# New orders for every engine's list and for the PSUM pairs of a fused gated SSM-convolution and mixer kernel

## The chip, the cores and the metric

The kernel runs on one core of one Trainium2 chip. The metric is the device time of one execution in microseconds (us), median of several runs; lower is better. The profile is one more execution, recorded by the hardware profiler. In its rows PE is the matrix engine (TensorE), PEld its weight loads, DVE the vector engine, ACT the scalar engine, POOL the GpSimd engine and SP the engine whose queue issues most DMA transfers; a q behind an engine's name is its sequencer, which waits and issues.

## The reference

```python
def _A_ref(q, k, v, shift_k, ssm_k, ssm_D):
    ...
    for t in range(ks):
        k_shift = k_shift + k_pad[:, t:t + S, :] * shift_k[:, ks - 1 - t][None, None, :]
    kv = k_shift * v
    ...   # y: causal convolution of kv with ssm_k along the sequence, through rfft / irfft
    y = y + kv * ssm_D[None, None, :]
    return q * y

def _B_ref(x, w1, w2, w3, w4):
    h = _gelu(_layernorm(x, axis=-1) @ w1)
    ...   # hs: four column groups of h shifted by +1, -1, +2, -2 rows, then @ w2
    x1 = x + hs
    h2 = _gelu(_layernorm(x1, axis=-1) @ w3) @ w4
    return x1 + h2

x = A_q
g = _sigmoid((x * gate_w).sum(-1, keepdims=True))
return g * a + (1 - g) * b      # a = _A_ref(x, ...), b = _B_ref(x, ...)
```

S is 2048, D 640, F 1536, all in bfloat16. Branch A is a gated long convolution; branch B is a two-layer mixer; a sigmoid gate per row mixes them.

## The kernel before, in words

The 2048 rows lie in SBUF as 2 blocks (c) x 8 residue classes (rho or r) x 128 partitions. Everything is written as 981 nodes, each one instruction or a short run of matmuls on one engine, with its reads and writes. `schedule(RANK, PAIR)` then sorts all nodes by a rank from a written-out table, `RANK`, and each engine works through its nodes in that order, without looking ahead. A node waits on semaphores for what it depends on on other engines; everything behind it on that engine waits too. So the table sets the order of each engine's list.

PSUM is four pairs of banks. Each matmul job (a node or two on PE, and the ACT or DVE instruction that evicts it) has its pair from a second table, `PAIR`. A job's first node waits until the job before it on that pair has been evicted.

The names of nodes that matter here, with the line that records the operation:

- fill: up to 96 matmuls on a tile of ones (L645), whose result nobody reads; those that are last in PE's list are dropped.
- shk: row broadcasts of the shift taps on PE (L656), evicted by ACT. gwt (L651) and gsum (L909) are small products for the gate, halo (L667) makes the rows before a block.
- bn (L776 statistics, L778 aggregate), ln (small DVE instructions at L554, L766, L768, L794) and the reciprocal root on POOL (L756): layer norm, once for x, once for x1. For the first, class 1 has its statistics from ACT. Classes 2 and 3, 4 and 5, 6 and 7 share a root. The second is in four groups, with row sums by ACT and squares by ACT (L566, with the accumulator read).
- xn: the normalised rows (DVE L554, or ACT L566 for most of the second norm). xTp (L821): transposition on PE of a class's normalised rows, evicted by ACT (xTe). Classes 6 and 7 of the first norm and all of the second are transposed by DMA from SP's queue.
- mm1 (L861): first product of B with gelu, by pairs of classes; the first pair is split into class 0 and class 1, each in three pieces. tail (L901): small DMAs from POOL's queue that shift the fifth column tile. mm2 (L971, seeded in PSUM by ACT at L953), mm3 (L1062, gelu on ACT) and mm4 (L1033, seeded) are the other products. The last group of mm4 is done in halves: one evicted by ACT, the other by DVE with an addition (L1046).
- kv: the four-tap convolution times v, on DVE (L549), in four parts. tap (L711): ssm_k transposed on PE. L721 is a small POOL addition of ssm_D to the taps; one comes early, one late.
- fwd (L1091): forward transform of taps (fwdh) and of kv (fwdk), for each half of the columns, evicted by ACT (Sh, Sk). DVE then does windows, butterflies, products and folds (L549), with some additions done by accumulating DMAs from POOL's queue (L1121). inv and inve (L1234) are the inverse transform, with eviction gy on ACT; fin and finx on DVE multiply by q and add to B's part.
- Stores to DRAM are issued by SP (L1273 and, for the last mm4 group, L1052), in list order.

Nearly all DVE additions and products show as L549, nearly all ACT evictions as L580, because one helper records them.

Of the kernel before, what the change touches and what calls it, by code (L numbers as in the profile page):

```python
# [292 lines left out]
def _bf16_bits(a):  # L293
# [34 lines left out]
R4M = {("h",1),("k",1)}  # L328
FILL = 96
RANK = [  # L330
# [46 lines left out]
]  # L377
PAIR = [
# [7 lines left out]
]  # L386

def _freq(kap):
# [962 lines left out]
```

## Time and profile before

| what | value |
|---|---|
| median of 3 runs | 223.71 us (223.3 to 223.88) |
| the profiled execution: time, span of its instructions | 222.89 us, 220.9 us |
| PE busy | 213.5 us, 97% |
| DVE busy | 205.9 us, 93% |
| ACT busy | 171.9 us, 78% |
| POOL busy | 58.4 us, 26% |
| granted TensorE clock | 1.00 of full speed |

Starts in the rows are microseconds from the start of the span. "[0.30 <-X]" behind a row is the time the engine stood idle before it and what ended that. Rows that follow each other on an engine with one line, operation and tile are merged (x3). Neighbouring instructions of DVE, ACT and PE overlap by about 0.1 us in the rows, since the next one starts before the last has drained.

### The profile page before, as it was taken

To read this page: it belongs to the slowest core of one execution; us is meant where nothing else is said; L and a number is where in the kernel's file an instruction comes from. 1 tells how busy PE (TensorE), PEld (TensorE's weight loads), DVE (VectorE), ACT (ScalarE), POOL (GpSimd) and SP (SyncE) were. 2 spreads that over 40 slices of the span, in tenths; PEclk is the share of its full clock that TensorE was granted. 3 is DMA by queue.
4 is the path that set the end of the run, shared out by engine and by line. 5 is a ranking of instruction groups with operands and counts; after the bars stand their busy time and mean duration, and the time that the engine had idled before them with its cause. 6 is when DMAs were issued, how large, how long until landed. Compare 5 with 4: busy or idle time off the path is not lost.

```text
span 220.9 us, 3934 instructions
## 1 busy us (share of the span) xinstructions
PE 213.5 (97%) x1531; PEld 135.5 (61%) x1531; DVE 205.9 (93%) x307; ACT 171.9 (78%) x291; POOL 58.4 (26%) x64
## 2 busy tenths in 40 slices
PE   8999999999989999999999999999999999999993
PEld 8769655557756645447765554466665577567771
DVE  2999999999999899999999999999999999984984
ACT  4798998889999999999998988855246552296561
POOL 1231780341202303490003110223231204138000
PEclk9999999999999999999999999999999999999999
DMA  6999999779976542967232450496976897798758
GB/s 216 380 399 367 360 286 188 292 151 238 184 215 197 161 82 39 346 115 235 57 59 59 74 107 0 76 156 116 184 125 119 128 323 146 141 207 117 134 159 259
DMA packets 41580, 39.76 MB, mean 180 GB/s; under 512 B 20453, under 2 KB 34792, under 8 KB 41433
## 3 DMA queue, kind: packets, MB, share of 16 engines
q1 hardware_dynamic: 33864, 24.75, 39.9%
q0 software_dynamic: 7408, 14.42, 32.3%
q10 hardware_dynamic: 288, 0.33, 0.6%
q8 instruction: 12, 0.20, 0.3%
q14 instruction: 8, 0.06, 0.1%
HBM read 21.60 MB, written 3.93 MB: 116 GB/s over the span
## 4 chain that ended last, share of the span: by engine, by line
PE 65%; DVE 19%; ACT 13%; issue 1%; DVEq 0%; ACTq 0%
PE PS L1033 23%; DVE arena L549 18%; PE PS L1062 18%; ACT arena L580 9%; PE PS L1234 7%; PE PS L1091 5%; PE PS L861 4%; PE PS L645 4%; ACT arena L566 3%; PE PS L821 2%; PE PS L711 1%; PE PS L656 1%; DVE arena L554 1%; ACT PS L953 1%; PE PS L667 0%
## 5 line engine op out<-in xcount | busy, mean ns | idle before, releaser
L549 DVE TENSOR_TENSOR arena<-arena 128x1280 bf16<-128x1280 bf16 (+5 forms) x212 | 182.8, 923 | 5.7 <-ACT arena L580 4.2
L580 ACT ACTIVATE arena<-PS 128x640 bf16<-128x640 f32 (+7 forms) x140 | 102.7, 794 | 19.6 <-PE PS L1062 11.5
L1033 PE MATMUL PS<-arena 128*128 128x320 bf16 x384 | 54.6, 299 | 0.3 <-ACT arena L580 0.3
L1062 PE MATMUL PS<-arena 128*128 128x512 bf16 x240 | 54.3, 379 | 0.1
L1033 PEld LDWEIGHTS PS<-arena 128*128 128x128 bf16 x384 | 37.5, 98 | 15.3 <-issue 0.6
L580 ACT ACTIVATE arena<-PS,arena 128x320 bf16<-128x320 f32 (+1 forms) x48 | 26.2, 594 | 21.5 <-PE PS L1033 17.2
L1121 POOL DMA_DIRECT2D arena<-arena x24 | 24.1, 1083 | 67.9 <-DVE arena L549 67.9
L1062 PEld LDWEIGHTS PS<-arena 128*128 128x128 bf16 x240 | 23.1, 98 | 26.8 <-issue 0.8
L1091 PE MATMUL PS<-arena 128*128 128x320 bf16 x208 | 33.1, 300 | 1.2 <-ACT arena L580 0.8
L1091 PEld LDWEIGHTS PS<-arena 128*128 128x128 bf16 x208 | 19.0, 98 | 13.7 <-ACT arena L580 4.4
L566 ACT ACTIVATE arena<-arena 128x640 bf16<-128x640 bf16 (+2 forms) x34 | 26.2, 776 | 1.6 <-DMA arena<-in_A_q_dram 1.2
L756 POOL TENSOR_TENSOR arena<-arena 128x4 f32<-128x4 f32 (+1 forms) x9 | 17.0, 1887 | 35.2 <-DVE arena L554 32.7
L971 PE MATMUL PS<-arena 128*128 128x320 bf16 x160 | 22.9, 299 | 1.0 <-ACT PS L953 1.0
L861 PE MATMUL PS<-arena 128*128 128x512 bf16 (+1 forms) x125 | 23.6, 336 | 0.0
L953 ACT ACTIVATE PS<-arena 128x640 f32<-128x640 bf16 x32 | 22.3, 714 | 0.3
L971 PEld LDWEIGHTS PS<-arena 128*128 128x128 bf16 x160 | 15.3, 98 | 7.7 <-issue 1.1
L861 PEld LDWEIGHTS PS<-arena 128*128 128x128 bf16 x125 | 11.7, 98 | 8.8 <-ACT arena L580 0.9
L1234 PE MATMUL PS<-arena 128*128 128x320 bf16 x112 | 17.0, 299 | 0.0
L776 DVE BATCH_NORM_STATS2 arena<-arena 128x6 f32<-128x320 bf16 x28 | 12.2, 477 | 3.4 <-DMA arena<-in_A_q_dram 3.3
L1234 PEld LDWEIGHTS PS<-arena 128*128 128x128 bf16 x112 | 10.9, 98 | 5.1 <-ACT arena L580 0.4
L901 POOL DMA_DIRECT2D arena<-arena x18 | 9.5, 536 | 9.6 <-ACT arena L580 9.6
L554 DVE TENSOR_SCALAR arena<-arena 128x640 bf16<-128x640 bf16 (+3 forms) x31 | 10.2, 349 | 1.3 <-POOL arena L756 0.8
(39 smaller groups left out, 66.0 us busy)
## 6 DMA issues: line engine op xcount, KB each, us to landing
arena<-arena POOLq DMA_DIRECT2D x18, 320.0 KB, 3.9
arena<-in_B_w_dram POOLq DMA_DIRECT2D x4, 960.0 KB, 7.1
arena<-in_A_k_dram SPq DMA_DIRECT2D x4, 640.0 KB, 7.0
arena<-in_A_v_dram SPq DMA_DIRECT2D x4, 640.0 KB, 12.9
arena<-arena POOLq DMA_DIRECT2D x4, 640.0 KB, 6.0
arena<-in_A_q_dram SPq DMA_DIRECT2D x4, 640.0 KB, 8.3
out_dram<-arena SPq DMA_DIRECT2D x15, 160.0 KB, 2.0
arena<-in_A_q_dram SPq DMA_DIRECT2D x6, 320.0 KB, 4.8
```

The source lines that it names most:

```text
L549: return dve(lambda e: e.tensor_tensor(o, a, b, op), [a, b], [o], c_tt(n), tag=tag, **kw)
L566: node = P.op("act", lambda e, ps: e.activation(o, i, func, **kw), r=r, w=[o], cost=c_act(n, naps, acc is not None, psum=False), tag=tag, ...
L580: node = P.op("act", lambda e, ps: e.activation(ov, inner(ps), func, **kw), r=r, w=[o], cost=c_act(n, len(r), acc is not None), job=job, t ...
L756: P.op("pool", lambda e, ps: e.tensor_tensor(r, v, hv, ALU.pow), r=[v, HALF], w=[r], cost=cost, tag="ln")
L861: fns.append(lambda e, ps, b=b, c=c, lhsT=lhsT: e.matmul(bank(ps, b, 256 * n), lhsT, XT[:, c, r0:r0 + n, :], start=(c == 0), stop=(c == 4)))
L953: P.seed(job, lambda e, ps: e.activation(two(ps, 320), x, ACTF.Copy), [X[:, c, rho, :]], c_act(640, psum=False), tag)
L971: fns.append(lambda e, ps, hh=hh, ft=ft, lhsT=lhsT: e.matmul(bank(ps, hh, 320), lhsT, w2v[:, ft, 320 * hh:320 * hh + 320], start=False, st ...
L1033: fns.append(lambda e, ps, hh=hh, ft=ft, lhsT=lhsT: e.matmul(bank(ps, hh, 320), lhsT, w4h[ft // 6][:, ft % 6, 320 * hh:320 * hh + 320], st ...
L1062: fns.append(lambda e, ps, b=b, ft=ft, c=c, sc=sc: e.matmul(bank(ps, b, 512), w3h[ft // 6][:, c, 128 * (ft % 6):128 * (ft % 6) + 128], XT[ ...
L1091: fns.append(lambda e, ps, w=w, b=b, rhs=rhs, st=(first and n == 0), en=(n == len(ss) - 1): e.matmul(bank(ps, b, 320), w, rhs, start=st, s ...
L1121: return P.dma("pool", lambda e, ps: e.dma_start(o, i, accum_op=ALU.add, max_dma_last_dim=2560), r=[o, i], w=[o], nbytes=nb, cost=1.2, kin ...
L1234: fns.append(lambda e, ps, w=w, z=z, c=c, st=(n == 0), en=(n == len(terms) - 1): e.matmul(bank(ps, c, 320), w, z[:, c, :], start=st, stop=en))
```

## The change

The two tables `RANK` (981 numbers) and `PAIR` (244 numbers) are replaced; the nodes, their instructions and what they read and write stay. The diff is these two tables and nothing else. Its first and last lines:

```diff
 RANK = [
-    978, 927, 967, 974, 980, 979, 966, 956, 951, 924, 932, 899, 887, 975, 938, 961, 808, 917, 797, 945, 794,
+    978, 937, 968, 975, 980, 979, 967, 952, 957, 931, 884, 924, 907, 976, 939, 962, 808, 874, 813, 946, 809,
...
 PAIR = [
-    3, 3, 3, 2, 3, 0, 0, 2, 2, 1, 2, 0, 0, 1, 1, 3, 2, 3, 1, 1, 2, 3, 1, 1, 3, 1, 2, 1, 2, 0, 3, 2, 3, 3, 3, 3,
+    2, 3, 3, 1, 1, 3, 0, 1, 1, 3, 0, 0, 0, 1, 2, 0, 2, 3, 2, 2, 3, 3, 1, 1, 2, 1, 3, 0, 0, 0, 0, 2, 0, 1, 0, 1,
...
```

Written out as lists (numbers behind a dot count the nodes of that name), these are the places that the prediction speaks of. PE's first entries:

```
before: fill x72, shk, fill x9, xTp class 0, fill x11, shk, gwt, halo 0, xTp class 1, halo 1, mm1 0a.0, mm1 0a.1, mm1 0b.2, gsum, shk, shk, mm1 0a.2, ...
after:  fill x70, shk, fill x11, shk, fill x2, gwt, xTp class 0, fill x3, halo 0, halo 1, xTp class 1, mm1 0a.0, mm1 0a.1, shk, mm1 0a.2, shk, mm1 0b.2, ...
```

DVE, from the input of the root of classes 4 and 5 on (ln 4, ln 6: inputs of the roots; statistics and aggregates are bn):

```
before: ln 4, bn x3, kv 0.1, bn, xn 5, bn x3, xn 5, bn x2, xn 4, ln 6, kv 0.0, xn 4, kv 0.2, memset, xn 6, xn 7, kv 0.3, xn 6, kv 0.4, xn 7, ...
after:  ln 4, kv 0.0, memset, bn (aggregate), xn 5, xn 5, kv 0.2, bn x2, xn 4, bn x2, xn 4, bn, ln 6, kv 0.3, memset, xn 7, xn 6, kv 0.4, xn 7, ...
```

ACT, from before the last gelu of the first mm3 group to mm4's third seed:

```
before: ..., square 3.0, gelu3, square 3.1, seed4, gelu3, Sh, gelu3, xn, seed4, xn, Sh, xn, xn, Sh, seed4, ...
after:  ..., seed4, square 3.0, gelu3, Sh, gelu3, square 3.1, seed4, Sh, xn, xn, xn, xn, Sh, Sh, seed4, ...
```

In the second norm, the reader of the root of classes 6 and 7 follows the root's input on DVE behind two butterfly instructions and a small one now, where it had four butterfly instructions and a small one before. Near the end, PE takes inve pieces 0 and 2 one behind the other after the last DVE-evicted half of a block's mm4; SP's list of stores begins with a store that needs a finx, and the two stores that went out first before are its third and twelfth now. POOL, SP and the pairs have other exchanges of neighbours.

102 rows, old and new, of tables (PAIR, RANK) are left out of this document.

## The prediction

> **What bounds the kernel now.** I read the page first (busy shares, then the chain that ended last), then the table by stage, the chain in order of time, and the timelines of single engines.
>
> ```profile
> PE 213.5 (97%) x1531; PEld 135.5 (61%) x1531; DVE 205.9 (93%) x307; ACT 171.9 (78%) x291; POOL 58.4 (26%) x64
> PE 65%; DVE 19%; ACT 13%; issue 1%; DVEq 0%; ACTq 0%
> ```
>
> PE is busy nearly always, but the chain runs through it for 65% only. The table by stage (from:to, its length; busy us and instructions of PE, PEld, DVE, ACT, POOL; granted clock, DMA share, GB/s) says where another engine is as full:
>
> ```profile
> 0.00:12.30 12.30, 11.24 (x126) 9.70 (x127) 8.23 (x30) 8.14 (x15) 2.75 (x8) 1.00 0.87 310
> 12.30:28.20 15.90, 15.90 (x166) 12.38 (x165) 15.14 (x42) 14.85 (x20) 7.13 (x7) 1.00 1.03 374
> 28.20:71.20 43.00, 41.83 (x337) 26.43 (x335) 42.50 (x30) 40.22 (x80) 12.67 (x20) 1.00 0.88 215
> 71.20:98.40 27.20, 26.25 (x151) 13.69 (x152) 26.20 (x45) 26.84 (x54) 10.64 (x8) 1.00 0.55 148
> 98.40:146.00 47.60, 47.15 (x284) 27.00 (x285) 47.29 (x63) 43.59 (x63) 6.37 (x6) 1.00 0.45 92
> 146.00:215.50 69.50, 69.50 (x466) 45.32 (x465) 64.26 (x97) 37.35 (x63) 18.80 (x19) 1.00 0.80 157
> ```
>
> From 28 to 98 us three engines are full at once. The chain in order of time (start, length, what) shows who hands over to whom:
>
> ```profile
> 1.06 6.72 PE PS L645 x72
> ...
> 8.44 0.61 PE PS L645 x9
> ...
> 9.60 0.61 PE PS L645 x11
> ...
> 28.19 1.30 DVE arena L554 x2
> ...
> 69.61 1.50 DVE arena L549
> ...
> 71.16 0.73 PE PS L1091 x4
> ...
> 71.92 1.90 ACT arena L580 x3
> ...
> 95.78 2.46 ACT arena L580 x3
> ...
> 98.37 3.42 PE PS L1033 x24
> ```
>
> So DVE decides until the last shift-convolution product ends at 71.11 (kv, L549), ACT until 98.2 (the last gelu before the first mm4), PE after that to 215.5. A list order can win only waits: no instruction is dropped but fillers. PE's idle inside 12.3 to 215.5 is 1.17 + 0.95 + 0.45 = 2.6 us (span less busy, rows three to five of the table); that and the six fillers (below) are all there is to gain before the tail.
>
> **The change, part by part.** I wrote both lists of every engine side by side, counted the work that stands ahead of each instruction in either (durations from the timelines), and looked where an input now comes after the place of its reader.
>
> *Fillers.* 92 of the L645 matmuls are issued now, 86 after. At 0.61/11 = 0.056 us each that is -0.34 us on PE, unless the next input is late. It is:
>
> ```profile
> 7.13 0.80 DVE L554 TENSOR_SCALAR arena<-arena 128x640 bf16<-128x640 bf16 x2
> 9.40 0.88 DVE L776 BATCH_NORM_STATS2 arena<-arena 128x6 f32<-128x320 bf16 x2
> 10.37 0.75 DVE L554 TENSOR_SCALAR arena<-arena 128x640 bf16<-128x640 bf16 x2
> 12.29 2.89 PE L861 MATMUL PS<-arena 128*128 128x256 bf16 x25
> ```
>
> The transposition of row class 1 stands ahead of the first mm1 piece in both lists, but DVE now does one statistics pass (0.40), one aggregate (0.11) and two memsets (0.14) more before it finishes class 1's normalised rows: 11.12 + 0.65 = 11.77 instead of 11.12. PE, 0.34 ahead, waits for it, and 0.56 of transposing later the first mm1 starts at 12.35 against 12.29. Both row broadcasts (L656) ahead of it are hidden in that wait. Net 0.0 on PE. With the cover gone (class 1 on time) it would be -0.3.
>
> *DVE to 71 us.* This is the term that matters, since DVE's end there releases fwdk. The reciprocal roots (L756) run on POOL between two DVE instructions:
>
> ```profile
> 17.94 0.49 DVE L776 BATCH_NORM_STATS2 arena<-arena 128x6 f32<-128x320 bf16 x1 [0.30 <-DMA arena<-in_A_q_dram]
> 18.58 1.01 POOL L756 TENSOR_TENSOR arena<-arena 128x4 f32<-128x4 f32 x1 [4.57 <-DVE arena L554]
> 20.99 0.20 DVE L778 BATCH_NORM_AGGREGATE arena<-arena 128x2 f32<-128x12 f32 x1
> 23.20 2.82 DVE L549 TENSOR_TENSOR arena<-arena 128x5120 bf16<-128x5120 bf16 x1
> 23.37 3.52 POOL L756 TENSOR_TENSOR arena<-arena 128x4 f32<-128x4 f32 x1 [3.79 <-DVE arena L554]
> 26.30 1.48 DVE L549 TENSOR_TENSOR arena<-arena 128x2560 bf16<-128x2560 bf16 x1
> 27.84 0.06 DVE L852 MEMSET arena<- 32x1 bf16 x1
> 28.19 1.30 DVE L554 TENSOR_SCALAR arena<-arena 128x640 bf16<-128x640 bf16 x2 [0.30 <-PE PS L821]
> 28.53 0.78 POOL L721 TENSOR_TENSOR arena<-arena 1x320 bf16<-1x320 bf16 x1
> 73.71 1.52 DVE L554 TENSOR_SCALAR arena<-arena 128x640 bf16<-128x640 bf16 x4 [0.85 <-POOL arena L756]
> 92.28 3.75 POOL L756 TENSOR_TENSOR arena<-arena 128x4 f32<-128x4 f32 x1
> ```
>
> The root takes 1.01 beside statistics passes, but 3.52 when a 2.82 us kv product starts just before it: it ends 26.89, 0.87 after the product's end at 26.02. In the old list a normalisation and the 1.48 kv step of 26.30 stand between, so nobody waits for that root. The new list has for classes 4 and 5: the root's input, the 2.82 us kv product, one memset (0.06), one aggregate (0.20 less the 0.08 by which DVE instructions overlap), and then the normalisation that needs the root. So DVE waits 0.87, plus 0.03 from POOL's end to DVE's start (73.68 to 73.71 in the row of 73.71, whose root is of the same kind), less 0.18 of small work, plus the 0.08 overlap: 0.80. For classes 6 and 7: input, a 1.48 kv step, one memset, then the reader: 0.87 + 0.03 - 0.06 + 0.08 = 0.92. Against that go the old list's own waits: 0.30 for a load (x now lands earlier), 0.30 for a transposition, 0.50 where POOL's L721 stretched two normalisations to 1.30 (0.80 at 7.13), and 0.1 of small ones. Moved work in that stretch adds 0.13. Sum 0.80 + 0.92 + 0.13 - 1.20 = +0.65: the last kv product ends at 71.76. Lower bound -0.3 (POOL slips in first and both waits vanish, the old 0.50 stays); upper bound +1.15 (L721 falls into a normalisation again). I take +0.65, nearest to the 3.52 row, which is the same pair of instructions in the same order.
>
> The Trainium skill (SBUF — State Buffer, "SBUF: two separate sides") gives the mechanism: DVE and GpSimd share one port pair, whichever starts first holds it for its whole instruction, and the other blocks. The 3.52 row agrees. By that rule alone a blocked root enters at the next instruction's end; at 92.28 it took 3.75 us beside instructions of 0.8 us, so by the row it can lose several rounds. The place where the two differ is classes 6 and 7 of the second norm (DVE about 115): by the rule its reader would wait 0.0, by the row up to 0.9, and the total would come out 0.0 or about 0.2 longer, since DVE has slack there.
>
> *ACT from 71 to 98.* fwdk starts about 71.8 instead of 71.16, so its first eviction is 0.6 late. But one square pass has been put behind the last gelu that mm4 waits for:
>
> ```profile
> 91.10 0.72 ACT L566 ACTIVATE arena<-arena 128x640 bf16<-128x640 bf16 x1
> 120.05 2.21 ACT L580 ACTIVATE arena<-PS 128x1024 bf16<-128x1024 f32 x3 [0.54 <-PE PS L1062]
> 134.70 1.62 ACT L580 ACTIVATE arena<-PS 128x1024 bf16<-128x1024 f32 x2 [0.64 <-PE PS L1062]
> 135.78 0.72 PE L1091 MATMUL PS<-arena 128*128 128x320 bf16 x4 [0.30 <-ACT arena L580]
> ```
>
> +0.6 - 0.72 = -0.1: mm4 begins at 98.25 against 98.37. PE could not be much earlier: the same work from 71.76 ends at 97.1.
>
> *98 to 146.* That square pass now stands between the gelu and everything ACT does next, so ACT is 0.6 to 0.75 behind its old place when it evicts, while PE is not. I walked the PSUM pairs by the ACT and PE timelines. An example: behind the last gelu ACT has the square (0.72), a seed, three Sh evictions, and four normalisations before mm4's third seed; that ends at 105.65, and PE stands there from 105.25. So mm4's third seed is 0.4 late, the mm3 behind Sh of the odd residue 0.35, the fwdk behind the 131 us gelu 0.55, and some 0.1s; PE's old idle here was 0.45 (the 0.30 at 135.78 among it), and ACT's own old waits (0.54, 0.64) take up most of its lag by 135. Net +0.7: inv begins 0.6 later than 145.3. Bounds: 0.0 (ACT's old waits absorb all) to +1.3 (each stall stands).
>
> *146 to the end.* PE's list is dense in both. One new wait: inve's second piece takes the PSUM pair of an mm4 half whose DVE eviction (0.55, L1046) ends 0.25 too late. PE ends about +0.9. The stores:
>
> ```profile
> 204.01 1.21 SPq L1273 DMA_DIRECT2D out_dram<-arena  x2
> 211.33 0.34 SPq L1052 DMA_DIRECT2D out_dram<-arena  x1
> 217.52 0.54 DVE L1046 SCALAR_TENSOR_TENSOR arena<-PS,arena 128x320 bf16<-128x320 f32 x1
> 218.49 0.49 SPq L1052 DMA_DIRECT2D out_dram<-arena  x1
> ```
>
> Now two stores go out at 204 and fifteen back to back from 211.33, (218.49 - 211.33)/14 = 0.51 each; the last one's data was ready at 218.06, so the queue is 0.4 late. After, all seventeen stand behind one finx that I place at 210.7, and 16 x 0.51 later is 218.9; the data is ready at 218.06 + 0.9 = 218.96. Last store +0.5.
>
> Sum on the profiled execution: 220.9 + 0.5 = 221.4 span; with the 1.99 around it (222.89 - 220.9) 223.4. The median of the runs is 223.71, 0.82 above the profiled one, so I carry +0.5 over: 224.2. About 0.3% (0.67 us) is what a measurement of this kernel tells from no change.
>
> **The rivals.** *Faster, the roots are not blocked.* If POOL gets in first both DVE waits go, fwdk starts at 71.2 and PE stays ahead by its 0.34 of fillers and some of its old 0.95 idle. The 18.58 row (1.01, unblocked) speaks for it, the 3.52 row against. PE would end 0.5 earlier, but the stores cap it: finx at 209.7, last store 217.9, so -0.6 at most: 223.1; with a little of the lag left 223.3. Chance 0.28.
>
> *Slower, ACT's lag is not recovered.* One mechanism, at 98 to 135: every PSUM pair that PE wants next is the one ACT evicts last, so PE inherits ACT's whole 0.75 and each of the stalls above (0.4 + 0.35 + 0.55) stands without the old 0.45 going. It decides if ACT shows no wait on PE until 135. PE ends +1.6, stores +1.2 to +1.5: 225.1. The old 0.54 and 0.64 waits speak against it. Chance 0.22.
>
> *Nothing changes.* The DVE lag is taken by the moved square pass, and the store queue decides the end in both: 223.7. Chance 0.12.
>
> **How the numbers follow.** Forecast (223.5 to 224.8 as its own range, 224.2 the middle): 0.38, of which two thirds lie within 0.3% of 223.71 (to 224.38). Faster by more than 0.3%: 0.17 of the first rival's 0.28, the rest within. Slower: the second rival's 0.22 and 0.12 of the forecast. Together faster 0.17, same 0.49, slower 0.34. The range 222.9 to 225.3 takes in the first rival's best and the second's usual case.
>
> **What the new profile would show.** Right: an L756 of about 3.6 and one of 2.3 between 20 and 31 us, each followed by an idle DVE for POOL of 0.8 to 0.9; PE idle of 0.5 or more before the first fwdk at about 71.8; the first mm4 near 98.3; ACT without the 0.54 at 120; seventeen stores in one row from about 210.7. Wrong: L756 near 1.0 there, fwdk at 71.2 or before, inv before 145.0. I would be wrong most easily in how the four PSUM pairs mesh between 98 and 135, where each stall is a few tenths and their sum decides the sign.

## The result and the profile after

The changed kernel takes 225.5 us in the median of 6 runs (225.26 to 226.68), beside 223.56 (6 runs, 223.3 to 224.0) of the kernel before on the same chip: ratio 1.0092, 95% interval 1.0068 to 1.0117. It is slower by about 2 us (1.94 between the medians, 2.06 by the ratio). The prediction was 224.2 with a range of 222.9 to 225.3, and "slower" had 0.34 of the chance.

The profiled execution took 225.44 us, its span is 223.6 (before 222.89 and 220.9). That is +2.7, more than the medians differ: the profiled run of the kernel before lay 0.8 below its median. I read places and sizes from the traces, and totals from the timed runs.

The page of the changed kernel, busy shares and the chain that ended last by engine:

```profile
PE 213.4 (95%) x1513; PEld 134.2 (60%) x1525; DVE 206.5 (92%) x307; ACT 171.8 (77%) x291; POOL 61.4 (27%) x64
PE 52%; DVE 28%; ACT 12%; POOL 2%; issue 2%; DMA 2%; DVEq 0%; ACTq 0%
```

PE is no busier than before. DVE's share of the chain went from 19% to 28%, but that share says little by itself: in the trace of the kernel with only its stores reordered (below), whose DVE list is the same, it is 7%. The table by stage (columns as in the prediction), with the bounds moved along with the events (28.20 is the same time in both):

```profile
0.00:12.50 12.50, 10.98 (x119) 8.92 (x120) 8.26 (x34) 8.11 (x15) 2.61 (x8) 1.00 0.86 297
12.50:28.20 15.70, 15.54 (x152) 11.34 (x151) 14.96 (x36) 14.63 (x19) 6.68 (x6) 1.00 1.03 398
28.20:72.50 44.30, 42.66 (x348) 26.98 (x348) 43.01 (x35) 40.93 (x81) 14.22 (x20) 1.00 0.91 206
72.50:99.20 26.70, 25.94 (x148) 13.78 (x151) 25.84 (x44) 25.90 (x51) 9.74 (x7) 1.00 0.53 147
99.20:146.50 47.30, 46.35 (x275) 26.63 (x280) 46.21 (x64) 44.08 (x65) 9.24 (x6) 1.00 0.48 88
146.50:217.00 70.50, 70.29 (x469) 45.63 (x470) 66.26 (x98) 38.19 (x64) 18.90 (x19) 1.00 0.80 154
```

The stage that ends with fwdk is 44.3 us long where it was 43.0 (28.20 to 71.20). The clock is 1.00 in every stage up to 217 us, so the clock has no part in this. The events one by one (us from the start of the span):

| event | before | predicted | after |
|---|---|---|---|
| first mm1 | 12.29 | 12.35 | 12.52 |
| last kv product ends | 71.11 | 71.76 | 72.49 |
| first fwdk | 71.16 | 71.8 | 72.55 |
| first mm4 | 98.37 | 98.25 | 99.22 |
| inv begins | 145.29 | 145.9 | 146.45 |
| PE ends | 217.14 | 218.0 | 218.64 |
| last DVE result | 218.06 | 218.96 | 219.23 |
| last store issued | 218.49 | 218.9 | 221.12 |

Two rows carry it: the last kv product is 1.38 late instead of 0.65, and the last store goes out 1.9 behind the last result. DVE's timeline between 20 and 34 us shows the first, with POOL's:

```profile
20.73 2.82 DVE L549 TENSOR_TENSOR arena<-arena 128x5120 bf16<-128x5120 bf16 x1
23.60 0.06 DVE L852 MEMSET arena<- 32x1 bf16 x1
23.68 0.21 DVE L778 BATCH_NORM_AGGREGATE arena<-arena 128x2 f32<-128x12 f32 x1
24.55 0.81 DVE L554 TENSOR_SCALAR arena<-arena 128x640 bf16<-128x640 bf16 x2 [0.67 <-POOL arena L756]
...
28.63 1.48 DVE L549 TENSOR_TENSOR arena<-arena 128x2560 bf16<-128x2560 bf16 x1
30.18 0.06 DVE L852 MEMSET arena<- 32x2 bf16 x1
31.12 0.80 DVE L554 TENSOR_SCALAR arena<-arena 128x640 bf16<-128x640 bf16 x2 [0.89 <-POOL arena L756]
31.84 2.08 DVE L549 TENSOR_TENSOR arena<-arena 128x2560 bf16<-128x2560 bf16 x1
```

```profile
20.91 3.54 POOL L756 TENSOR_TENSOR arena<-arena 128x4 f32<-128x4 f32 x1 [1.32 <-DVE arena L554]
28.82 2.20 POOL L756 TENSOR_TENSOR arena<-arena 128x4 f32<-128x4 f32 x1 [3.08 <-DVE arena L554]
31.70 0.86 POOL L721 TENSOR_TENSOR arena<-arena 1x320 bf16<-1x320 bf16 x1
```

The two waits are there, 0.67 and 0.89. A third loss was not in the sum: the kv step at 31.84 takes 2.08 where its like at 28.63 takes 1.48, with POOL's L721 running from 31.70 to 32.56 beside it.

The second loss, in the timeline of SP's queue (start, how long SP took to issue, line):

```profile
211.34 0.40 SPq L1273 DMA_DIRECT2D out_dram<-arena  x1
211.78 1.98 SPq L1052 DMA_DIRECT2D out_dram<-arena  x1
213.80 0.94 SPq L1273 DMA_DIRECT2D out_dram<-arena  x2
...
221.12 0.50 SPq L1052 DMA_DIRECT2D out_dram<-arena  x1
```

Seventeen stores stand in one row behind the finx that ends at 211.31, and the second takes 1.98 us instead of about 0.5. Six of them go out between 198.99 and 209.47 when they stand first (next section).

### The profile page after: what moved, and what is told of

Its sections match the earlier page's. It is cut to its first block, busy times and chain, and to the rows that moved or that the text cites. A ratio compares the mean times of both kernels' runs of the same rounds, so it can differ in the third digit from the quotient of the medians.

```text
span 223.6 us, 3915 instructions
## 1 busy us (share of the span) xinstructions
PE 213.4 (95%) x1513; PEld 134.2 (60%) x1525; DVE 206.5 (92%) x307; ACT 171.8 (77%) x291; POOL 61.4 (27%) x64
## 4 chain that ended last, share of the span: by engine, by line
PE 52%; DVE 28%; ACT 12%; POOL 2%; issue 2%; DMA 2%; DVEq 0%; ACTq 0%
DVE arena L549 23%; PE PS L1033 16%; PE PS L1062 13%; PE PS L861 9%; ACT arena L580 7%; PE PS L1234 6%; PE PS L1091 5%; ACT PS L953 3%; POOL arena L756 2%; DVE arena L776 2%; ACT arena L566 2%; DMA arena<-in_A_q_dram 2%; DVE arena L554 2%; PE PS L711 1%; PE PS L821 1%
## 5 line engine op out<-in xcount | busy, mean ns | idle before, releaser
L580 ACT ACTIVATE arena<-PS 128x640 bf16<-128x640 f32 (+8 forms) x140 | 102.3, 799 | 15.6 <-PE PS L1062 7.3
L1062 PE MATMUL PS<-arena 128*128 128x512 bf16 x232 | 53.1, 379 | 0.9 <-ACT arena L580 0.3
L756 POOL TENSOR_TENSOR arena<-arena 128x4 f32<-128x4 f32 (+1 forms) x9 | 20.1, 2236 | 28.2 <-DVE arena L554 26.3
L861 PE MATMUL PS<-arena 128*128 128x512 bf16 (+1 forms) x121 | 22.9, 335 | 0.3 <-issue 0.2
L953 ACT ACTIVATE PS<-arena 128x640 f32<-128x640 bf16 x32 | 22.9, 719 | 0.3
L971 PE MATMUL PS<-arena 128*128 128x320 bf16 x160 | 22.9, 299 | 0.2 <-ACT PS L953 0.2
L971 PEld LDWEIGHTS PS<-arena 128*128 128x128 bf16 x160 | 15.3, 98 | 6.9 <-ACT PS L953 0.8
```

The costliest lines, as they stand in the source:

```text
L580: node = P.op("act", lambda e, ps: e.activation(ov, inner(ps), func, **kw), r=r, w=[o], cost=c_act(n, len(r), acc is not None), job=job, t ...
L756: P.op("pool", lambda e, ps: e.tensor_tensor(r, v, hv, ALU.pow), r=[v, HALF], w=[r], cost=cost, tag="ln")
L861: fns.append(lambda e, ps, b=b, c=c, lhsT=lhsT: e.matmul(bank(ps, b, 256 * n), lhsT, XT[:, c, r0:r0 + n, :], start=(c == 0), stop=(c == 4)))
L953: P.seed(job, lambda e, ps: e.activation(two(ps, 320), x, ACTF.Copy), [X[:, c, rho, :]], c_act(640, psum=False), tag)
L971: fns.append(lambda e, ps, hh=hh, ft=ft, lhsT=lhsT: e.matmul(bank(ps, hh, 320), lhsT, w2v[:, ft, 320 * hh:320 * hh + 320], start=False, st ...
L1062: fns.append(lambda e, ps, b=b, ft=ft, c=c, sc=sc: e.matmul(bank(ps, b, 512), w3h[ft // 6][:, c, 128 * (ft % 6):128 * (ft % 6) + 128], XT[ ...
```

## The experiments

The theory has two terms: DVE's two waits for the roots (with the kv step beside L721) push everything from fwdk on, and the row of stores adds its own delay at the end. The main rival is the prediction's second one: the time is lost between 98 and 146, where PE's pairs mesh with a late ACT.

In the list diffs, "out c.n" is a store at L1273, "outl 3.n" one at L1052, kvb the last two steps of a kv part (sum and product with v), and "sq" the square pass. Only the ranks behind such a list were renumbered. Every kernel was timed beside the kernel before, whose medians were 223.4 to 223.8 us, so the ratios to it are what I compare.

**Stores in the order of readiness.**

```diff
 SP, behind the last load
-out 1.2, outl 3.4, out 0.3, out 0.2, outl 3.3, out 0.4, outl 3.2, out 0.0, out 0.1, out 1.1, ..., outl 3.0
+out 0.2, out 0.0, out 0.1, out 0.3, out 0.4, out 0.5, outl 3.4, out 1.2, outl 3.2, out 1.0, ..., outl 3.0
```

> The changed kernel with one list altered: the seventeen stores on SP's queue stand in the order in which their data is ready in its trace (six that are ready by 208.5 us first), everything else as it is. Theory (the queue of stores sets the end): the last store is issued at 219.3, right behind the last DVE result at 219.23, instead of 221.12, and lands about 221.2 instead of 223.1: -1.8 us, 223.7 against 225.5. First rival (PE and DVE set the end, the queue is only beside it): less than 0.4 us is gained, 225.1 or more. Second rival (stores at 199 to 209 take DMA time from the accumulating additions on POOL's queue that finish B's part): the additions land later, a finx waits, and 0.5 to 1.0 is gained: 224.5 to 225.0.

Measured: 223.49 us, ratio 0.9997 (0.9984 to 1.001), against 1.0092 without the edit. SP's queue in this kernel:

```profile
198.99 10.86 SPq L1273 DMA_DIRECT2D out_dram<-arena  x6
...
212.62 1.22 SPq L1273 DMA_DIRECT2D out_dram<-arena  x1
...
219.32 0.34 SPq L1052 DMA_DIRECT2D out_dram<-arena  x1
```

The last store goes out at 219.32, right behind the last result at 219.29. PE's end did not move (218.71 beside 218.64). So the order of the stores alone cost some 2 us: 1.5 of it is the second store's stall, which goes to the end because everything stands behind it, and without it the row would have ended at 219.6, 0.4 behind the last result. The second rival here (early stores delay the additions) falls: the finx that 1.2 waits for ended at 211.38, against 211.31 without the edit.

**DVE without the two waits.**

```diff
 DVE, from the input of the root of classes 4 and 5 (ln 4) on
-ln 4, kv 0.0, memset, bn, xn 5, xn 5, kv 0.2, bn x2, xn 4, bn x2, xn 4, bn, ln 6, kv 0.3, memset, xn 7, xn 6, kv 0.4
+ln 4, bn x6, xn 5, xn 5, ln 6, xn 4, xn 4, kv 0.0, memset, kv 0.2, kv 0.3, memset, xn 7, xn 6, kv 0.4
```

> The changed kernel with DVE's list altered between 20.7 and 34 us alone: behind each root's input stand statistics and normalisations now, and the first 2.82 us kv product comes only behind both inputs, so that no DVE instruction waits for POOL's root. Theory (DVE's two waits of 0.67 and 0.88 pass through fwdk to the end): last kv product ends at about 71.0 instead of 72.49, first fwdk 71.1, first mm4 at about 97.9 instead of 99.22, finx of class 1.2 and with it the first store 1.2 earlier: 224.3 against 225.5. Rival (the time is lost in the meshing of PSUM pairs between 98 and 146, and an earlier fwdk only makes PE wait there): last kv product as in the theory, but first mm4 or inv gain less than 0.4: 225.1 or more.

Measured: 224.39 us, ratio 1.0032 (1.002 to 1.0045). DVE and POOL in this kernel:

```profile
21.43 0.15 DVE L554 TENSOR_SCALAR arena<-arena 128x4 f32<-128x4 f32 x1
...
24.32 2.82 DVE L549 TENSOR_TENSOR arena<-arena 128x5120 bf16<-128x5120 bf16 x1
27.27 3.49 DVE L549 TENSOR_TENSOR arena<-arena 128x2560 bf16<-128x2560 bf16 x2
30.89 0.80 DVE L554 TENSOR_SCALAR arena<-arena 128x640 bf16<-128x640 bf16 x2
```

```profile
21.67 1.04 POOL L756 TENSOR_TENSOR arena<-arena 128x4 f32<-128x4 f32 x1 [1.32 <-DVE arena L554]
26.52 1.51 POOL L756 TENSOR_TENSOR arena<-arena 128x4 f32<-128x4 f32 x1
28.61 0.79 POOL L721 TENSOR_TENSOR arena<-arena 1x320 bf16<-1x320 bf16 x1
```

Beside statistics the root takes 1.04 instead of 3.54, and no DVE row before 74 us names L756 any more. L721 found another kv step (the two of 27.27 take 3.49, where two of 1.48 that overlap by 0.08 take 2.88). The time came out as the theory had it, but the trace less cleanly: the loads of this profiled run came late (first mm1 13.28), and the last kv product ended at 71.66, not 71.0.

**Both repairs.**

> Both edits together: DVE's list between 20.7 and 34 us without the two waits, and the stores in the order of readiness. Theory (two terms that add): -1.8 and -1.2, 222.5, which is below the kernel before. Rival (both take away the same wait at the end): no better than the better of the two, about 223.7.

Measured: 222.60 us, ratio 0.9952 (0.9936 to 0.9969), below the kernel before. The terms nearly add: from 1.0092, the stores took off 0.0095, DVE's order 0.0060, both 0.0140. Against the kernel with the stores alone, whose first mm1 is 0.3 later, the last kv product moved from 72.75 to 71.47, mm4 from 99.48 to 98.54, inv from 146.53 to 145.59 and PE's end from 218.71 to 217.78. So of 1.28 us at the last kv product 0.94 arrive at mm4, and from there 0.93 at the end; 0.29 of each is the earlier first mm1. The rest has no way to show: PE starts fwdk at 71.64, 0.17 behind the last kv product and without a wait for it. The chain that ended last runs through ACT from 50.3 to 80.1 us, where with the stores alone it left ACT at 69.5 for DVE's last kv instructions.

**The stores' order alone, on the kernel before.**

```diff
 SP, behind the last load
-out 0.5, out 0.3, outl 3.2, out 0.0, out 0.1, outl 3.3, out 1.1, outl 3.4, out 0.4, out 1.2, ..., outl 3.0
+out 1.2, outl 3.4, out 0.3, out 0.2, outl 3.3, out 0.4, outl 3.2, out 0.0, out 0.1, out 1.1, ..., outl 3.0
```

> The kernel before with one list altered: its seventeen stores in the order of the changed kernel, all behind the finx that was done at 213.06 us in its trace. Theory (the queue sets the end, at 0.53 us a store): the last store is issued 16 x 0.53 later, at 221.6, or at 223.1 if the second store stalls for 1.98 us as in the changed kernel, against 218.49: +3.1 to +4.6, 226.7 to 228.2. Rival (the stores' order does not matter, PE sets the end): within 0.4 of 223.6.

Measured: 226.34 us, ratio 1.0118 (1.0103 to 1.0134), +2.5, a little under the theory's +3.1. In its queue:

```profile
213.67 0.40 SPq L1273 DMA_DIRECT2D out_dram<-arena  x1
214.11 0.47 SPq L1052 DMA_DIRECT2D out_dram<-arena  x1
...
221.96 0.50 SPq L1052 DMA_DIRECT2D out_dram<-arena  x1
```

The last store starts at 221.96, 16 x 0.52 behind the first. The queue sets the end, as in the theory, and the rival falls. The second store does not stall here (0.47), which says that the 1.98 does not belong to the order of the stores as such. What it may belong to is below.

**The kernel before with its stores in the order of readiness.**

```diff
 SP, behind the last load
-out 0.5, out 0.3, outl 3.2, out 0.0, out 0.1, ..., out 0.2, out 1.4, outl 3.0
+out 0.3, out 0.4, out 0.5, out 0.0, out 0.1, out 0.2, outl 3.3, outl 3.4, outl 3.2, ..., out 1.4, outl 3.0
```

> The kernel before with its seventeen stores in the order in which their data is ready in its own trace; all else as it is. Theory (in the kernel before the queue was late by little): the last store goes out at about 218.1 us, behind the last DVE result at 218.06, instead of 218.49: -0.4 us, 223.4 where the kernel before has 223.8. Rival (only PE sets the end of the kernel before): no change.

Measured: 223.14 us, ratio 0.9983 (0.9966 to 1.0). In its trace the last store goes out 0.03 behind the last result, where it was 0.43, but at 218.58 instead of 218.49, since in this execution everything from the first mm1 on is 0.3 to 0.5 later. The size agrees in the timed runs, but the interval reaches to no change.

**L721 on fewer columns.** On the kernel with the stores in order:

```diff
-e.tensor_tensor(t0row, t0row, DROW[h], ALU.add)
+e.tensor_tensor(t0row[:, 0:8], t0row[:, 0:8], DROW[h][:, 0:8], ALU.add)
```

> The changed kernel with the stores in the order of readiness, and POOL's two additions of ssm_D to the taps (L721) done on 8 of 320 columns; the other columns get no ssm_D. Theory (the addition on POOL stretches the kv instruction of DVE beside it): the kv instructions that took 2.08 us, at 31.8 and 61.7, take 1.48 each, the last kv product ends 1.2 earlier than with the stores alone altered (71.5 instead of 72.75), and the time is 222.5 instead of 223.49. Rival (something else stretches them, the transfers that land in SBUF then for instance): both stay at 2.08 and the time at 223.5.

Measured: 222.56 us, ratio 0.9956 (0.9939 to 0.9972), where the kernel with the stores alone had 0.9997. The kv step and POOL beside it (lines behind L721 stand one further down in this kernel):

```profile
31.34 0.80 DVE L554 TENSOR_SCALAR arena<-arena 128x640 bf16<-128x640 bf16 x2 [0.88 <-POOL arena L757]
32.06 1.48 DVE L549 TENSOR_TENSOR arena<-arena 128x2560 bf16<-128x2560 bf16 x1
```

```profile
31.92 1.68 POOL L721 TENSOR_TENSOR arena<-arena 1x8 bf16<-1x8 bf16 x1
```

Both kv steps are back at 1.48 and the last kv product ends at 71.52, 1.23 earlier, 0.60 for each: L721 was the cause. POOL itself took longer (1.68 instead of 0.86), so now it seems to wait for DVE, and not DVE for it. The two waits for the roots are still here (0.88 in the row above), and yet the time is that of the version without them (222.60): fwdk starts at 71.67, again without a wait for DVE. Either of DVE's losses, taken away alone, gives about the same, since DVE no longer decides then.

**The square pass put back.** On the version with both repairs:

```diff
 ACT, at the last gelu ahead of mm4
-..., Sh 3.6, gelu3, sq 3.1, seed4 0.3, ...
+..., Sh 3.6, sq 3.1, gelu3, seed4 0.3, ...
```

> The changed kernel with both repairs (DVE without the two waits, stores in the order of readiness), and the square pass that the change put behind the last gelu ahead of mm4 put back ahead of it. Theory (the prediction's step: the moved square is worth its 0.72 us at mm4, and costs part of it again until inv): first mm4 at 99.2 instead of 98.54, inv 0.0 to 0.4 later, 222.6 to 223.0 against 222.60. Rival (PE sets the start of mm4): first mm4 within 0.1 of 98.54.

Measured: 223.16 us, ratio 0.9981 (0.9969 to 0.9994), 0.0029 worse. PE's wait for the gelu at mm4:

```profile
99.72 3.42 PE L1033 MATMUL PS<-arena 128*128 128x320 bf16 x24 [0.72 <-ACT arena L580]
```

From the first fwdk to mm4 it is 27.51 us against 26.90 with the square behind the gelu, and to inv 74.56 against 73.95: +0.61 at both. So the square behind the gelu is a gain of 0.6 in this version, kept to the end; nothing of it is paid back between 98 and 146. PE's two waits of 0.34 for ACT in that stage (below) are there with the square in either place, so the moved square is not their cause.

**DVE's order alone, on the kernel before.** From the input of the root of classes 4 and 5 to the last kv step of part 0, in the order of the changed kernel, with the stores in order of readiness:

```diff
 DVE, from ln 4 on
-ln 4, bn x3, kv 0.1, bn, xn 5, bn x3, xn 5, bn x2, xn 4, ln 6, kv 0.0, xn 4, kv 0.2, memset, xn 6, ...
+bn x2, kv 0.1, bn, ln 4, kv 0.0, memset, bn, xn 5, xn 5, kv 0.2, bn x2, xn 4, bn x2, xn 4, bn, ln 6, kv 0.3, xn 7, ...
```

> The kernel before with its stores in the order of readiness (which took 223.14 us), and with DVE's list from the input of the root of classes 4 and 5 to the last kv step of part 0 in the order of the changed kernel: one part of the change done alone. Theory (the order on DVE there is what costs, whatever list stands around it): DVE waits for POOL's roots 0.7 and 0.9 us, the first of the two kv steps beside L721 takes 2.08 instead of 1.48, the last kv product ends at about 72.7 instead of 71.58, and the time is 224.0. Rival (the waits cost only together with the changed lists of PE and ACT): last kv product later too, but the time within 0.3 of 223.14.

Measured: 226.21 us (five runs, 225.82 to 230.58), ratio 1.0125 (1.0105 to 1.0146): about 3 us more than the same without it, and neither theory nor rival said so much. DVE has its two waits (0.64 and 0.97) and the last kv product ends at 73.39 instead of 71.58. L721 did not fall on a kv step, as the theory had it, but on a normalisation (0.91 at 34.23, where the next takes 0.43). But PE lost more. Its waits in the trace:

```profile
29.57 0.72 PE L821 MATMUL PS<-arena 128*128 128x128 bf16 x10 [1.20 <-DVE arena L778]
43.54 1.24 PE L861 MATMUL PS<-arena 128*128 128x512 bf16 x5 [1.92 <-DMA arena<-arena]
```

The old list of PE transposes class 4 and starts the mm1 of classes 6 and 7 (transposed by DMA) where the old DVE order had their rows ready. With the rows later, PE stands at both, becomes the one that ends last, and fwdk starts at 74.75. The changed list of PE has two forward transforms ahead of class 4's transposition, and no wait there. The price of an order on one engine depends on the lists beside it.

**Further along the same line.** On the version with both repairs, DVE's list again:

```diff
-..., kv 0.1, bn x4, ln 4, bn x6, xn 5, ...; kv 1.1, kv 1.2; kv 2.1, kv 2.2; kvb 3.0, kvb 3.1
+memsets first; ..., bn x2, ln 4, bn x4, kv 0.1, bn x4, xn 5, ...; kv 1.1, gate, kv 1.2; kv 2.1, kvb 1.1, kv 2.2; kvb 3.0, ln 4.4, kvb 3.1
```

> The changed kernel with both repairs and more on DVE's list: the six small memsets go to its start, where DVE waits for the first load; four statistics and the input of the root of classes 4 and 5 go ahead of the first kv product; and three instructions are put between kv steps that depend on each other (the gate's between two steps of part 1, the last product of part 1 between two steps of part 2, the input of the second norm's first root between the two last kv products). Theory (DVE's end at 71 still sets the end, one to one up to PE's idle of some 2 us): last kv product at about 70.5 instead of 71.47, first mm4 at 97.6, 221.7 against 222.60. Rival (from there on PE or the loads decide): last kv product as in the theory, but less than 0.4 gained in all: 222.2 or more.

Measured: 222.27 us, ratio 0.9937 (0.9922 to 0.9952), the best of all. The rival's case came, DVE no longer decides: the last kv product ends at 70.30, 1.17 earlier, but only 0.34 of it reaches the time. In the trace DVE and PE at the end of that stage (the first 1.49 of the DVE row are the last kv product):

```profile
68.81 3.09 DVE L549 TENSOR_TENSOR arena<-arena 128x2560 bf16<-128x2560 bf16 x3
```

```profile
67.73 3.56 PE L971 MATMUL PS<-arena 128*128 128x320 bf16 x25
71.12 1.87 PE L1091 MATMUL PS<-arena 128*128 128x320 bf16 x12
```

PE has mm2 (L971) to do until 71.12 and starts fwdk without a wait. By the chain that ended last it is not PE's own work alone that bounds the stage: the chain runs through PE to 42.8, through ACT from 49.8 to 79.6, and only then through PE again.

One step more, at the front:

```diff
 DVE, class 1
-..., bn, bn, xn 1, bn, xn 1, ...
+..., bn, xn 1, xn 1, bn, bn, ...
```

> The version of 222.27 us, with the normalised rows of class 1 ahead of one statistics pass and one aggregate more. Theory (PE decides in this version up to 72 us, since its first fwdk starts 0.8 after the last kv product): the first mm1 starts at 11.85, when its weights land, instead of 12.21, and fwdk 0.35 earlier: 221.9. Rival (ACT, full from the first eviction on, decides): first mm1 earlier, fwdk at 71.0 or later, no gain: 222.2 or more.

Measured: 222.23 us, ratio 0.9947 (0.9932 to 0.9963), not to be told from the last. First mm1 12.06, fwdk 70.97: only 0.15 of the 0.36 came at the first mm1, and all of it arrived at fwdk, which starts 58.91 behind the first mm1 in both versions. So the time fits the rival and the trace the theory, and the run does not decide between them: in its chain PE stands up to 42.6 us and ACT from 49.7 to 79.4.

## Why the prediction was wrong, step by step

*Fillers and front:* PE waited for class 1 as said (0.46 idle), first mm1 12.52 instead of 12.35, without effect here, since DVE comes last at fwdk (PE waited 0.94 for it).

*DVE to 71, predicted +0.65, measured +1.38.* The two waits were forecast at 0.80 and 0.92 with the lost overlap of 0.08 in each; 0.67 and 0.89 are 0.75 and 0.97 with it. The 3.54 and 2.20 of the roots are the forecast 3.6 and 2.3. The step that failed is L721: the sum took off the old 0.50 that it cost and let it cost nothing in its new place. It fell on a kv step and cost 0.60 (the L721 experiment). The late L721 cancels: it costs a kv step 0.6 in both kernels (3.41 instead of 2.82 at 60.36 in the kernel before). That is most of the missing 0.73; the last 0.13 or so was not traced. The upper bound had L721 in it, at 1.15, and was still too low: both the waits and L721 came. The lower bound of -0.3 does not follow from its own terms: without the two waits and with the old 0.50 the sum is -0.57.

The Trainium skill's rule (SBUF — State Buffer, "SBUF: two separate sides") was to be decided by the root of classes 6 and 7 in the second norm. The chain that ended last has it now, and DVE's timeline the reader:

```profile
114.31 2.96 POOL arena L756
```

```profile
114.14 2.22 DVE L549 TENSOR_TENSOR arena<-arena 128x1280 bf16<-128x1280 bf16 x2
116.28 0.20 DVE L554 TENSOR_SCALAR arena<-arena 128x16 f32<-128x16 f32 x1
117.29 0.17 DVE L800 SCALAR_TENSOR_TENSOR arena<-arena 128x4 f32<-128x4 f32 x1 [0.82 <-POOL arena L756]
```

In this trace the reader waited 0.82 for it, near the 0.9 of the row and not the 0.0 that the prediction drew from the rule: POOL did not get in at 114.96, when the first of the two products of 114.14 ended, but by its end only behind the second, at 116.36. Three blocked roots (24.45, 31.02, 117.27) each end 0.90 behind the end of a long DVE instruction (23.55, 30.11, 116.36). But the seven other traces of the changed lists, in which DVE and POOL have the same order here, show the other case. The kernel with the stores reordered:

```profile
114.57 1.51 POOL L756 TENSOR_TENSOR arena<-arena 128x4 f32<-128x4 f32 x1 [12.70 <-DVE arena L554]
```

```profile
114.40 2.22 DVE L549 TENSOR_TENSOR arena<-arena 128x1280 bf16<-128x1280 bf16 x2
116.54 0.16 DVE L554 TENSOR_SCALAR arena<-arena 128x16 f32<-128x16 f32 x1
116.62 0.15 DVE L800 SCALAR_TENSOR_TENSOR arena<-arena 128x4 f32<-128x4 f32 x1
```

There the root took 1.51, ended 0.86 behind the first product, and nobody waited. So one order gives both, and the case is not settled: a blocked root gets in behind the first or behind the second DVE instruction, and no run shows which of the two it will be.

*ACT, 71 to 98:* predicted -0.75 from fwdk to mm4 by the moved square, measured -0.54 (26.67 instead of 27.21), and 0.61 in the experiment. Mechanism right. The 97.1 that the prediction gives for PE's own work does not follow from its table: 71.76 and the 26.25 us that PE is busy there make 98.0.

*98 to 146, predicted +0.7, measured +0.31.* PE's waits of a tenth or more in this stage are these two, where the old list had 0.12 and 0.30:

```profile
115.48 2.10 PE L1062 MATMUL PS<-arena 128*128 128x512 bf16 x9 [0.34 <-ACT arena L580]
132.95 1.31 PE L1091 MATMUL PS<-arena 128*128 128x320 bf16 x8 [0.35 <-ACT arena L580]
```

Two of the three named stalls came (mm3 behind Sh 0.34 for 0.35, fwdk behind the gelu 0.35 for 0.55), and the one at mm4's third seed did not. The cause that the prediction gave for them, an ACT late by the square, is wrong: with the square ahead of the gelu they are 0.34 each, and the stage is as long (47.05). Of the +0.31, 0.18 belongs to this trace alone, where the chain runs from the late root at 114.31 through DVE and ACT to PE's wait at 132.95: in the seven other traces of the changed lists the stage is 47.05 long, +0.13. The second rival falls with it: it came near the right total by the wrong place.

*146 to the end:* predicted +0.3, measured +0.33; inve's two pieces at 211.13 took 1.53 where their like take 1.25, which is 0.28 for the forecast 0.25, and the weight load of the second (211.94) waited for L1046, as said.

*The stores, predicted +0.5 at the last one, measured +2.63.* This is the larger failure. I placed the first of the seventeen at 210.7 and the last 16 x 0.51 later, at 218.9, which would have been level with the data. The first went out at 211.34 (0.64 later; PE was 0.55 later than forecast at inv, by DVE's term), the second took 1.51 more than a step, and the rest 0.1. A row with no slack has no room for one stall: each tenth by which finx is late, and each stall, goes to the end in full.

So the two steps that failed are costs that the sum left out: L721 in its new place (0.60), and a row of stores without slack (1.5 for one stall, 0.6 for the late start). The waits and the order of stores were read rightly from the lists, and so was the sign; both terms were sized at the point where they just did not hurt. Of the other rivals, "the roots are not blocked" falls with the 3.54 row, and "nothing changes" because the moved square took back only 0.54 of the 1.39 by which fwdk was late, and the queue of stores cost more than before.

## What to carry to other kernels

Sort the stores by when their data is ready, and let nothing that is ready early stand behind something late: here it was worth 2 us of 224 where the change had put all seventeen behind one result, and 0.4 at most in the kernel before; it touched no engine. When an order moves a small instruction of an engine that shares something with another (here POOL's roots and L721), charge it at its new place, and do not only take it off at its old one. Between the input of such an instruction and its reader, leave work for as long as it takes when blocked (3.5 us here), not when free (1.0). And ask which engine bounds the stage once the first is repaired: here 1.28 us less on DVE gave 0.9, and a further 1.17 us gave 0.34.

## What the hardware showed

*A store that stalls.* The DMA view of the changed kernel between 211 and 213 us (queue, packets, MB, share of 16 engines; below it the store issued there, with us to landing), and of the kernel before with the same stores between 211 and 212.5, ahead of its first store, which landed after 2.0:

```profile
q8 instruction: 1, 0.02, 4.8%
out_dram<-arena SPq DMA_DIRECT2D x1, 160.0 KB, 3.4
```

```profile
q8 instruction: 1, 0.02, 5.0%
```

An instruction block of 0.02 MB is loaded in both, in one piece: 4.8% of 16 engines over 2 us is 1.5 us on one DMA engine. In the changed kernel it lies under the first two stores: the first landed 3.4 us after its issue, and the second held SP for 1.98. In the other it lies ahead of the first store (213.67), and the second store took 0.47. In the kernel with the stores in order the same load meets the store at 212.62, which took 1.22, where nobody waits. The Trainium skill (Runtime: NRT & Kernel Launch, "Instruction fetch mechanics") says that instructions come in blocks of 16 KiB over a DMA queue of their own, at a cost that is mostly hidden; the size agrees to the two decimals shown, and here a cost seems to have shown on a neighbour. The link rests on where the loads lie in these traces; no run moved the load itself.

*Who waits at L721.* With 320 columns POOL took 0.86 and DVE's instruction 0.60 more; with 8 columns POOL took 1.68 and DVE nothing more.
